# One order table for every engine's share of a piece, a PSUM bank table, and one copy for the gate transposes

## The chip, the cores and the metric

The kernel runs on one core of a Trainium2 chip. Its time is the device time of one execution in microseconds. Five engines work in parallel, each through its own queue in program order: TensorE (PE in the profile, its weight loads PEld), VectorE (DVE), ScalarE (ACT), GpSimd (POOL) and SyncE (SP), which here issues the DMAs.

## The reference

The first half is a recurrence over 768 time steps for 4 batches of 8 heads, with a state of 40 by 40 for each. The second half is a gated MLP with a spatial mixing matrix over the 768 positions.

```python
for t in range(S):
    y[:, :, t] = np.einsum('bhd,bhde->bhe', rt, state)
    Sa = np.einsum('bhde,bhe->bhd', state, at)
    state_decay = state * wt[:, :, None, :] - np.einsum('bhd,bhe->bhde', Sa, bt)
    state = state_decay + np.einsum('bhd,bhe->bhde', vt, kt)
...
h = x @ w_in
h = 0.5 * h * (1.0 + np.tanh(c * (h + 0.044715 * h ** 3)))
u, v = (h[..., :d_ff // 2], h[..., d_ff // 2:])
v_n = (v - mu) / np.sqrt(var + 1e-06) * g_ln
v_s = np.einsum('ts,bsd->btd', w_sg, v_n) + b_sg[None, :, None]
return (x + (u * v_s) @ w_out).astype(np.float32)
```

## The kernel before

**Attention.** The recurrence is cut into 12 chunks of 64 steps, and a chunk into 4 batches b. For each chunk and batch the gates are made by eight pieces (lines 252 to 309): `gate_1` a scan of the decays (ex), `gate_2` the product at, a copy of it on ScalarE and a copy of the last decays (`call`) on GpSimd, `gate_3` and `gate_b` the scaled keys kb, `gate_4` the 16 score products into two PSUM banks and the four transposes of kb into the free halves of the same banks, `gate_a` the masked scores, `gate_n` their negated part (nts), `gate_k` two ScalarE copies of the transposes into kbt.

A chunk then needs the inverse of a triangular matrix of 32 by 32 blocks. `inv_in` (line 311) transposes nts into n and copies the identity into x; `steps` (line 320) are 31 steps of a product (tg) and a sum (x), each needing the one before. All but the last few steps run on GpSimd; `LASTS` says for each chunk how many go to VectorE. `train` (line 567) lays them out: the first `HALF` instructions of a chunk's train follow each other, the remaining ones alternate with the start of the next chunk's train. `inv_back`, `inv_g` and `inv_x` make the inverse of the 64 by 64 matrix (tiles x1z, xt, gp, xp).

The chunk itself is `chain1` to `chain5` (lines 425 to 509): products with the state (ru), with the inverse (ru again, vu), the new state (`chain3`: sp, 16 products of 32 columns of weights; `chain3b`: sc, vs), the outputs (pq, pqs, yp, yt) and their stores to xd in DRAM.

**MLP.** The weights come as 64-bit numbers. Each of 12 blocks of w_in and 8 of w_out is decoded by `split64` (line 711): a DMA into one of three staging buffers (stg), Abs on ScalarE (sc), four VectorE operations, two ScalarE operations (lt and the high half), and three operations for the low half on GpSimd or VectorE (`DEC`). Then for each batch `in_v` and `in_u` make products (hv, hu) and gelu (tiles p and q, six buffers shared by all of them and by sc and lt), `sgu` the spatial mixing (sg, g, split into gy and gx), `outp` the output (op, y). `product` issues the matmuls of one product; the other engines' share follows at lags given to `later` and is run by `tick`.

**The order.** Every instruction stands in its engine's queue in the order in which the program issues it (line 126 is where all of them are recorded, so every row of the profile has that line). The pieces of the attention and the early pieces of the MLP are put into a list with positions from hand-written tables (`CH`, `GPOS`, `DEC`, `DECO`, `START`, `BACK`), the list is sorted, and each piece is then run whole, so that all engines get their share of it at that point:

```python
        def merge(*lists):
            for _, f in sorted((x for l in lists for x in l), key=lambda x: x[0]):
                f()
```

PSUM has eight banks of 512 numbers for each partition. Six are taken in rotation by `Banks`, and two hold scan operands until the gates are done, after which the rotation is over eight.

Of the kernel before, what the change touches and what calls it, by code (L numbers as in the profile page):

```python
# [9 lines left out]
F32 = mybir.dt.float32  # L10
# [8 lines left out]
C = 64  # L19
# [8 lines left out]
RING = 18  # L28
# [3 lines left out]
GROWTH = 34  # L32
# [9 lines left out]
CH = ((0.15, 1.92, 4, 5.28, 4.96, 7.81, 8.16, 8.46, 12.17, 12.47, 3.28, 10.6, 13.17, 14.9), (-0.13, 1.6, 7.06, 5.51,  # L42
    8.56, 6.96, 8.97, 9.27, 11.23, 11.29, 2.43, 6.58, 12.67, 13.85))
GPOS = (((5.05, 5.33, 6.03, 6.08, 8.35, 10.4, 10.41, 10.42), (8.01, 8.01, 8.01, 9.58, 11.74, 11.88, 11.88, 11.89),
# [7 lines left out]
BACK = (23.33, 25.65, 29.14, 26)  # L52
# [5 lines left out]
DSTEP = ((-9.0, -1.0, 0.0, 0.7, 1.35, 2.4), (-9.0, -1.0, 0.0, 2.16, 3.15, 3.15))  # L58
# [10 lines left out]
FIRSTS = ('v0', 'v1', 'v2', 'u1', 'u0', 'u3', 'u2', 'v3', 'v4', 'v5', 'u4', 'u5', 'u7', 'u6')  # L69
# [3 lines left out]
REST = 8  # L73
SGS = (5, 5, 6, 6, 7, 8, 8, 11, 10, 11, 12, 11)
PO = 313.2
DECO = (332.78, 334.78, 336.78, 339.28, 340.91, 351.01, 348.0, 347.78)
DSTEPO = (-4.0, -1.0, 0.0, 0.7, 1.4, 2.4)
SGE = 'GGGGGVGVVVVV'
# [5 lines left out]
LASTS = (9, 0, 0, 0, 2, 1, 2, 1, 1, 1, 2, 2)  # L84
BEGIN = (14.05, 14.1, 14.15, 14.2, 14.3, 14.4, 14.5, 14.6, 14.7)
# [8 lines left out]
EX = ((0, 0.3, 0.6, 0.61, 1.5, 2.45, 2.46, 2.89), (0, 0.3, 0.6, 0.61, 1.5, 2.6, 2.61, 2.62))  # L94
class Banks:


    def __init__(self, tc, ctx):
        self.tc, self.ctx, self.n = tc, ctx, 0
        self.rings = [ctx.enter_context(tc.tile_pool(name="ps", bufs=6, space=PSUM))] * 6  # L100
# [6 lines left out]
    def grow(self):  # L107
        if len(self.rings) == 6:
            self.rings += [self.ctx.enter_context(self.tc.tile_pool(name="ps_more", bufs=2, space=PSUM))] * 2
# [1033 lines left out]
```

## Time and profile before

| | us |
|---|---|
| median of 3 runs | 642.31 (641.55 to 644.67) |
| the execution with the profile | 644.61 |
| its span, first to last instruction | 642.9 |
| busy in the span: TensorE | 546.6 |
| VectorE | 503.5 |
| ScalarE | 375.7 |
| GpSimd | 385.1 |

A busy time is the time in which an engine has an instruction under way; a wait is idle time before an instruction, put down to what released it. A row of a timeline that ends in x2 merges two instructions that follow each other. The chain that ended last is followed back from the last instruction, at each step to what released it.

### The profile page before, as it was taken

To read this page: it belongs to the slowest core of one execution; us is meant where nothing else is said; L and a number is where in the kernel's file an instruction comes from. 1 tells how busy PE (TensorE), PEld (TensorE's weight loads), DVE (VectorE), ACT (ScalarE), POOL (GpSimd) and SP (SyncE) were. 2 spreads that over 40 slices of the span, in tenths; PEclk is the share of its full clock that TensorE was granted. 3 is DMA by queue.
4 is the path that set the end of the run, shared out by engine and by line. 5 is a ranking of instruction groups with operands and counts; after the bars stand their busy time and mean duration, and the time that the engine had idled before them with its cause. 6 is when DMAs were issued, how large, how long until landed. Compare 5 with 4: busy or idle time off the path is not lost.

```text
span 642.9 us, 26868 instructions
## 1 busy us (share of the span) xinstructions
PE 546.6 (85%) x11190; PEld 486.6 (76%) x11190; DVE 503.5 (78%) x1061; ACT 375.7 (58%) x1058; POOL 385.1 (60%) x917
## 2 busy tenths in 40 slices
PE   6526888889898898888897965879999999999995
PEld 6315667777777786777786755779999999999995
DVE  7858888889898897888788769785689878668633
ACT  4526787787977788777776734653344345334400
POOL 5588688888888888788884555634241423343220
PEclk8556799999999998999887986969999999999999
DMA  8822334444444443433344242230016213000001
GB/s 258 240 63 64 95 101 113 115 122 120 109 112 114 125 127 95 109 97 101 83 139 141 76 140 67 90 110 8 25 44 196 87 57 104 1 32 12 19 32 37
DMA packets 60515, 60.77 MB, mean 95 GB/s; under 512 B 36256, under 2 KB 50336, under 8 KB 60384
## 3 DMA queue, kind: packets, MB, share of 16 engines
q1 hardware_dynamic: 60384, 58.96, 32.5%
q8 instruction: 90, 1.47, 1.0%
q14 instruction: 41, 0.34, 0.2%
HBM read 51.07 MB, written 7.86 MB: 92 GB/s over the span
## 4 chain that ended last, share of the span: by engine, by line
PE 59%; DVE 20%; issue 7%; ACT 7%; POOL 4%; DMA 2%; DVEq 0%; SPq 0%; POOLq 0%; ACTq 0%
PE sg L126 16%; PE op L126 7%; PE ab L126 6%; PE pq L126 5%; PE hu L126 5%; PE hv L126 5%; PE yp L126 5%; PE ru L126 4%; DVE sc L126 3%; DVE at L126 2%; DVE fixed L126 2%; PE sp L126 2%; DVE stg L126 2%; POOL x L126 1%; PE ut L126 1%
## 5 line engine op out<-in xcount | busy, mean ns | idle before, releaser
L126 POOL TENSOR_TENSOR tg<-x,n 128x96 f32<-128x96 f32 (+15 forms) x351 | 130.5, 375 | 40.0 <-DVE fixed L126 7.3
L126 POOL TENSOR_TENSOR x<-x,tg 128x96 f32<-128x96 f32 (+15 forms) x351 | 133.5, 384 | 22.2
L126 POOL TENSOR_TENSOR gx<-g,gy 128x384 fp32r<-128x384 f32 x31 | 32.1, 1038 | 89.8 <-ACT gy L126 89.8
L126 PE MATMUL sg<-wsh,vh 128*128 128x384 f32 x192 | 66.3, 345 | 3.1 <-ACT vh L126 3.1
L126 PE MATMUL sg<-wsh,vl 128*128 128x384 f32 x192 | 66.6, 347 | 2.7 <-POOL vl L126 2.7
L126 ACT ACTIVATE nts<-ab 32x256 f32<-32x256 f32 x192 | 62.2, 324 | 9.9 <-DVE at L126 7.4
L126 PE MATMUL sg<-wsl,vh 128*128 128x384 f32 x192 | 65.9, 343 | 0.0
L126 PE MATMUL yp<-pqs,kbt 128*64 128x64 f32 x768 | 51.1, 235 | 14.6 <-DVE pqs L126 12.1
L126 PE MATMUL pq<-rt,vut 128*128 128x128 f32 x384 | 59.0, 299 | 1.5 <-issue 1.3
L126 PE MATMUL ab<-at,kb 64*64 64x64 f32 x1536 | 42.8, 244 | 20.1 <-DVE kb L126 9.9
L126 ACT CAST gy<-g 128x384 fp32r<-128x384 f32 x32 | 16.4, 514 | 74.2 <-DVE g L126 74.2
L126 PEld LDWEIGHTS ab<-at,kb 64*64 64x64 f32 x1536 | 34.2, 151 | 28.2 <-issue 8.5
L126 PEld LDWEIGHTS yp<-pqs,kbt 128*64 128x64 f32 x768 | 40.6, 145 | 17.8 <-DVE pqs L126 11.9
L126 PEld LDWEIGHTS pq<-rt,vut 128*128 128x128 f32 x384 | 49.9, 202 | 4.8 <-issue 1.8
L126 DVE TENSOR_TENSOR at<-ab,mask 64x256 f32<-64x256 f32 x96 | 36.0, 410 | 18.4 <-PE ab L126 18.0
L126 ACT CAST vh<-v 128x512 fp32r<-128x512 f32 x24 | 14.9, 620 | 57.2 <-DVE v L126 57.2
L126 PE MATMUL yp<-rt,s 80*40 80x64 f32 x704 | 47.0, 230 | 0.7 <-issue 0.7
L126 POOL TENSOR_TENSOR vl<-v,vh 128x512 fp32r<-128x512 f32 x24 | 31.3, 1306 | 22.6 <-ACT vh L126 22.6
L126 DVE SCALAR_TENSOR_TENSOR g<-sg,gl,bt 128x384 f32<-128x384 f32 x32 | 19.7, 615 | 28.1 <-PE sg L126 26.2
L126 ACT COPY vs<-sc 64x160 f32<-64x160 f32 x88 | 28.3, 321 | 21.1 <-DVE sc L126 20.2
L126 PEld LDWEIGHTS sg<-wsh,vh 128*128 128x128 f32 x192 | 37.0, 193 | 4.1 <-ACT vh L126 3.8
L126 PEld LDWEIGHTS sg<-wsh,vl 128*128 128x128 f32 x192 | 37.0, 192 | 3.9 <-POOL vl L126 3.9
(137 smaller groups left out, 1533.3 us busy)
## 6 DMA issues: line engine op xcount, KB each, us to landing
main<-main SPq DMA_DIRECT2D x88, 160.8 KB
vu<-vs SPq DMA_DIRECT2D x24, 160.0 KB
vs<-vb SPq DMA_DIRECT2D x24, 160.0 KB
rt<-rt SPq DMA_DIRECT2D x48, 80.0 KB
vut<-vt SPq DMA_DIRECT2D x24, 160.0 KB
xd<-yt SPq DMA_DIRECT2D x96, 40.0 KB
ws<-seq_w SPq DMA_DIRECT2D x20, 192.0 KB
xt<-xd SPq DMA_DIRECT2D x16, 192.0 KB
```

Source lines behind the costliest of these rows:

```text
L126: return self.tc.keep_in_program_order(f(*a, **k))
```

## The change

Each piece is cut into the shares of its engines, written as generators or lists of functions. `Plan.put` names each share, and `ORDER` gives every name a rank: 3862 entries from the first gate to the last output. `Plan.run` sorts by rank. So a share of VectorE can stand far from the TensorE share of the same piece, and instructions of two trains, the copies of decays, DMA issues and the four parts of `chain5` have places of their own. `BANKS` names the PSUM bank of each allocation in turn.

`gate_4` keeps the 16 score products; the four transposes become `gate_t` with a bank of their own, which `gate_k` reads with one copy. `chain3` makes 8 products of 64 columns of weights instead of 16 of 32. The tiles p and q of gelu get two buffers each (`PB`), sc and lt four of half the size (`CB`). Some of the lists change: `LASTS`, `HALF`, `AE` (one product at goes to GpSimd), `CLAMPO` (three clamps go to GpSimd), `GROWTH`, and positions.

In `ORDER`, the train instructions are the entries sp (products) and ss (sums); the decoding is wi and wo, whose low halves stand behind the last train instruction (rank 2516, from rank 2553 on); the shares of `chain4` and `chain5` are c4 and c5. The mask of the last chunk's last batches has ranks 2954 and 2988, the first step behind Square of the three filler products 2955, 2963 and 2995, their products 2892, 2896 and 2965 among the last chunk's outputs (2887 to 3008). The low halves of the two w_out blocks 5 and 6 end at 3280 and 3281, behind the first spatial products (3167 and 3168). The table and the functions that are only cut into shares are shortened here:

```diff
-GROWTH = 34
+GROWTH = 37
...
-DEC = ((270.96, 0), (275.26, 0), (280.96, 0), (285.42, 0), (296.05, 1), (295.96, 0), (300.96, 0), (305.96, 1),
+DEC = ((270.96, 0), (275.26, 0), (280.96, 0), (285.42, 0), (295.34, 1), (295.96, 0), (300.96, 0), (305.96, 1),
...
-CLAMPO = (0, 0, 0, 0, 0, 0, 0, 0)
+CLAMPO = (0, 1, 0, 0, 1, 1, 0, 0)
...
-DECO = (332.78, 334.78, 336.78, 339.28, 340.91, 351.01, 348.0, 347.78)
+DECO = (332.78, 334.78, 336.78, 339.28, 340.91, 348.2, 348.0, 347.78)
...
-LASTS = (9, 0, 0, 0, 2, 1, 2, 1, 1, 1, 2, 2)
+LASTS = (11, 0, 0, 0, 2, 0, 0, 1, 1, 1, 2, 2)
...
-AE = ('VVV', 'VVV', 'V', 'V')
-HALF = (40, 54, 54, 54, 54, 54, 53, 53, 52, 54, 54, 54)
-LEAD = (0, 0, 0, 0, 0, 0, 0, 0, 0, 0, 0, 0, 0)
+AE = ('VVG', 'VVV', 'V', 'V')
+HALF = (40, 54, 51, 51, 52, 54, 52, 53, 49, 54, 51, 54)
+LEAD = (0, 0, 0, 0, 0, 0, 0, 3, 0, 0, 0, 0, 0)
...
+PB, CB = 2, 4
+INTRO, LATE = -100, 500
+V_AT = ((0, 5), (0, 6), (1, 5.5), (1, 6.5), (1, 7), (1, 8), (1, 9), (1, 9), (2, 7.5), (2, 10), (2, 10))
+U_AT = ((0, 5), (0, 6), (1, 5.5), (1, 6.5))
+S_AT = ((0, 6),) * 4
+O_AT = ((0, 6),) * 2
+L_AT = ((-1, 0), (-1, 0), (-1, 0), (-1, 0), (-1, 0), (-1, 0), (-1, 0), (-1, 0), (-1, 0), (-1, 0), (-1, 0))
+ORDER = {
+    "g0": (0, 13, 37, 43, 82, 84, 139, 147, 266, 187, 279, 282, 320, 433, 461, 471, 512, 514, 696, 741, 716, 717,
...
+    "sp": (90, 92, 94, 96, 99, 101, 103, 105, 107, 109, 111, 113, 115, 117, 119, 121, 123, 125, 127, 129, 201,
...
+        1532, 1534, 1536, 1538, 1540, 1542, 1545, 1549, 1554, 1556, 1551, 1560, 1553, 1564, 1559, 1568, 1563,
...
+    "ss": (91, 93, 95, 98, 100, 102, 104, 106, 108, 110, 112, 114, 116, 118, 120, 122, 124, 126, 128, 202, 203,
...
+        1533, 1535, 1537, 1539, 1541, 1543, 1547, 1550, 1555, 1558, 1552, 1561, 1557, 1566, 1562, 1570, 1565,
...
+    "ni": (75, 89, 190, 200, 357, 364, 579, 587, 794, 795, 1063, 1070, 1287, 1302, 1492, 1493, 1724, 1734, 1951,
...
+    "vl": (3696,),
+    "rest": (3050, 3153),
...
+    "l1": (3850, 3851, 3852, 3853, 3854, 3855, 3856, 3857, 3858, 3859, 3860, 3861),
+}
...
+BANKS = ("0123450301253534125053210205435104132514513014253045213501420143015130124515240303251404325043125242"
...
+        k = int(self.order[self.n]) if self.n < len(self.order) else self.n % len(self.pools)
         self.n += 1
-        return self.rings[self.n % len(self.rings)].tile([128, 512], F32, tag="ps", name=nm)
+        return self.pools[k].tile([128, 512], F32, tag=f"bank{k}", name=nm)
...
+class Plan:
+
+
+    def __init__(self, order):
+        self.items, self.order = [], order
+
+    def put(self, pos, key, *fs):
+        self.items += [(pos, f"{key}.{k}", f) for k, f in enumerate(fs)]
+
+    def parts(self, pos, key, n, g, *a, **kw):
+
+        run = []
+
+        def part():
+            if not run:
+                run.append(g(*a, **kw))
+            next(run[0], None)
+
+        self.put(pos, key, *[part] * n)
+
+    def run(self):
+        ranks = {k: iter(v) for k, v in self.order.items()}
+        todo = [(next(ranks[key.split(".")[0]]) if ranks else pos, f) for pos, key, f in self.items]
+        for _, f in sorted(todo, key=lambda x: x[0]):
+            f()
...
-            ab = gate[c, b] = ps("ab0"), ps("ab1")
...
+    def banks(c, b):
+        if (c, b) not in scores:
+            scores[c, b] = ps("ab0"), ps("ab1")
+        return scores[c, b]
...
+    def gate_4(c, b):
+        kb, at, ab = gate[c, b], ats[ent(c, b)], banks(c, b)
+        for p in range(NP):
             for h in range(2):
-                V.tensor_tensor(out=at[0:64, :, h], in0=ab[h][0:64, 0:256].rearrange("p (q x) -> p q x", x=C),
-                                in1=mask[0:64].unsqueeze(1).broadcast_to([64, NP, C]), op=ALU.mult)
-
-        def gate_n(c, b):
-            nt, q0 = nts[c % 3], 4 * b
-            for h in range(2):
-                r, abv = 64 * h, gate[c, b][h][:, 0:256].rearrange("p (q x) -> p q x", q=NP)
+                r = slice(64 * h, 64 * h + 64)
+                for x in range(2):
+                    T.matmul(ab[h][64 * x:64 * x + 64, C * p:C * p + C], lhsT=kb[r, p, x], rhs=at[r, p, 1],
+                             start=True, stop=True, tile_position=(64 * h, 64 * x), skip_group_check=True)
+
+    def gate_t(c, b):
+        kb, kt = gate[c, b], ps("kt")
+        kts[c, b] = kt
+        for p in range(NP):
+            T.transpose(out=kt[:, 128 * p:128 * p + 128], in_=kb[:, p], identity=ident)
...
-        def gate_k(c, b):
-            for g in range(2):
-                A.copy(out=kbts[ent(c, b)][:, 160 * g:160 * g + 160].rearrange("p (q h x) -> p q h x", q=2, h=2),
-                       in_=gate[c, b][g][:, 256:512].rearrange("p (q h x) -> p q h x", q=2, h=2)[:, :, :, 0:D])
...
+    def gate_k(c, b):
+        A.copy(out=kbts[ent(c, b)][:, 0:DM].rearrange("p (q h x) -> p q h x", q=NP, h=2),
+               in_=kts.pop((c, b)).rearrange("p (q h x) -> p q h x", q=NP, h=2)[:, :, :, 0:D])
...
-        def chain3(c, b):
-            kbt, vu, sc = kbts[ent(c, b)], vus[b // 2][:, b % 2], scs[b]
-            if c < NCH - 1:
-                sp = ps("sp")
-                for p in range(NP):
-                    for x in range(4):
-                        h, r = x // 2, slice(32 * x, 32 * x + 32)
-                        l0 = 2 * D * p + D * h + 32 * (x % 2)
-                        T.matmul(sp[r, D * p:D * p + D], lhsT=kbt[:, l0:l0 + 32],
-                                 rhs=vu[:, p // 2, h, p % 2], start=True, stop=True, tile_position=(0, r.start))
-                ts = sums[b] = sp[0:e, 0:NP * D].rearrange("p (q x) -> p q x", x=D)
-                V.tensor_tensor(out=ts, in0=ts, in1=sc[0:e], op=ALU.add)
...
+    def chain3(c, b):
+        kbt, vu, sc = kbts[ent(c, b)], vus[b // 2][:, b % 2], scs[b]
+        sp = ps("sp")
+        for p in range(NP):
+            for h in range(2):
+                r, l0 = slice(64 * h, 64 * h + 64), 2 * D * p + D * h
+                T.matmul(sp[r, D * p:D * p + D], lhsT=kbt[:, l0:l0 + 64], rhs=vu[:, p // 2, h, p % 2],
+                         start=True, stop=True, tile_position=(0, r.start), skip_group_check=True)
+        ts = sums[c, b] = sp[0:e, 0:NP * D].rearrange("p (q x) -> p q x", x=D)
+        yield
+        V.tensor_tensor(out=ts, in0=ts, in1=sc[0:e], op=ALU.add)
...
+    PIECES = ((gate_1, 0), (gate_2, -1), (gate_3, 0), (gate_b, 2), (gate_4, 0), (gate_a, -1), (gate_n, -1), (gate_k, 0))
...
-        return self.sb.tile([128, HF], dt, name=nm, tag="pq", bufs=6)[:, 0:n]
+        if nm in ("p", "q"):
+            return self.pv.tile([128, HF], dt, name=nm, bufs=PB)[:, 0:n]
+        return self.sb.tile([128, HF // 2], dt, name=nm, tag="c", bufs=CB)[:, 0:n]
...
+    def work(self, plan, x, b, n, pos):
+
+        k = int(x[1])
+        g, a, steps = {"v": (self.in_v, (b, k), V_AT), "u": (self.in_u, (b, k % 4, k // 4), U_AT),
+                       "s": (self.sgu, (b, k % 4, k // 4), S_AT), "o": (self.outp, (b, k % 3, k // 3), O_AT),
+                       "l": (self.last_outs, (b, k), L_AT)}[x[0]]
+        run = []
+
+        def part():
+            if not run:
+                run.append(g(*a))
+            next(run[0], None)
+
+        plan.put(pos, f"{x}.{b}.m", part)
+        for i, (lag, rank) in enumerate(steps):
+            plan.put(self.late(n + lag) + 0.05 + 0.04 * rank if lag >= 0 else pos + 0.001 * i, f"{x}.{b}.{i}", part)
...
+        plan = Plan(ORDER)
+        verdict = attention(tc, a, xd, flag, keep, ps, plan)
+
+        def check(wm):
+            part.last = verdict(wm)
+
+        part.lay_out(plan, True, check)
+        plan.run()
+        part.ctx.close()
```

## Rows read from the trace of the kernel before

**Rows 1.** Busy time of each engine in four stages (window: length, then busy us of each).

```profile
21.35:62.00 40.65, 19.03 (x478) 15.27 (x478) 30.44 (x71) 18.81 (x58) 34.38 (x93) 0.52 0.38 99
62.00:345.60 283.60, 246.25 (x8548) 207.39 (x8548) 241.14 (x516) 222.29 (x691) 234.98 (x658) 0.97 0.42 110
345.60:423.50 77.90, 56.72 (x841) 48.91 (x841) 60.49 (x136) 45.02 (x121) 41.83 (x58) 0.82 0.37 106
423.50:635.80 212.30, 212.25 (x1153) 204.41 (x1153) 154.79 (x306) 78.84 (x159) 65.23 (x67) 0.99 0.17 52
```

**Rows 2.** Who GpSimd waited for, from 21 to 346 us (us, times, longest).

```profile
POOL tg L126 <- DVE n L126: 5.4, 5, 2.0
POOL tg L126 <- ACT rhsb L126: 4.5, 1, 4.5
```

**Rows 3.** Groups of GpSimd instructions, 21 to 346 us (busy, mean ns, idle before).

```profile
L126 POOL TENSOR_TENSOR x<-x,tg 128x96 f32<-128x96 f32 (+15 forms) x351 | 133.5, 384 | 22.2
L126 POOL TENSOR_TENSOR tg<-x,n 128x96 f32<-128x96 f32 (+15 forms) x351 | 130.5, 375 | 40.0 <-DVE fixed L126 7.3 <-DVE n L126 5.4 <-ACT rhsb L126 4.5
```

**Rows 4.** Timeline of GpSimd, one train alone (start, us).

```profile
22.08 0.24 POOL L126 TENSOR_TENSOR tg<-x,n 128x30 f32<-128x30 f32 x1
22.40 0.24 POOL L126 TENSOR_TENSOR x<-x,tg 128x30 f32<-128x30 f32 x1
```

**Rows 5.** Timeline of GpSimd, two trains in alternation.

```profile
73.63 0.48 POOL L126 TENSOR_TENSOR tg<-x,n 128x30 f32<-128x30 f32 x2
74.07 0.49 POOL L126 TENSOR_TENSOR x<-x,tg 128x30 f32<-128x30 f32 x2
```

**Rows 6.** Timeline of GpSimd, the end of chunk 0's train.

```profile
40.26 0.60 POOL L126 TENSOR_TENSOR tg<-x,n 128x121 f32<-128x121 f32 x2
...
42.62 0.29 POOL L126 TENSOR_TENSOR tg<-x,n 128x58 f32<-128x58 f32 x1
```

**Rows 7.** Timeline of GpSimd, the copies of decays.

```profile
152.34 0.56 POOL L126 COPY call<-ex 128x4 f32<-128x4 f32 x4
```

**Rows 8.** Timeline of GpSimd, decoding inside the last train.

```profile
341.56 0.88 POOL L126 TENSOR_TENSOR lt<-lt,sc 128x256 f32<-128x256 f32 x1
...
344.09 0.33 POOL L126 TENSOR_TENSOR tg<-x,n 128x56 f32<-128x56 f32 x1
```

**Rows 9.** Timeline of GpSimd, a product at made there.

```profile
8.23 0.68 POOL L126 TENSOR_TENSOR at<-main,ex 128x256 f32<-128x256 f32 x1
```

**Rows 10.** Who TensorE waited for, from 62 to 346 us.

```profile
PE ru L126 <- issue: 8.1, 11, 1.3
...
PE gp L126 <- DVE x1z L126: 3.7, 3, 2.8
...
PE sp L126 <- issue: 2.0, 2, 1.5
PE ab L126 <- ACT kbt L126: 1.8, 1, 1.8
```

**Rows 11.** The chain that ended last, in order of time (start, us, what).

```profile
227.83 1.07 PE yp L126 x32
...
236.10 0.42 PE sp L126 x32
```

**Rows 12.** Groups by shape: the copy of a gate's transposes (busy, mean ns, idle before).

```profile
L126 ACT COPY kbt<-ab 128x160 f32<-128x160 f32 x96 | 23.4, 295 | 0.7
```

**Rows 13.** Who VectorE waited for, from 346 to 424 us.

```profile
DVE sc L126 <- ACT sc L126: 6.2, 2, 4.4
DVE q L126 <- ACT p L126: 4.9, 6, 1.2
```

**Rows 14.** Timeline of TensorE, the last chunk's last output.

```profile
392.50 0.48 PE L126 MATMUL yp<-pqs,kbt 128*64 128x64 f32 x4 [7.40 <-DVE pqs L126]
```

**Rows 15.** Groups by shape: Square of a v and the step behind it.

```profile
L126 DVE SCALAR_TENSOR_TENSOR q<-p,hv 128x512 f32<-128x512 f32 x24 | 16.4, 682 | 10.4 <-ACT p L126 10.4
...
L126 ACT ACTIVATE p<-hv 128x512 f32<-128x512 f32 x24 | 14.3, 598 | 4.0 <-PE hv L126 2.8 <-POOL wol L126 1.0
```

More of the change, by code (lines that the diff above doesn't have):

```diff
@@ L51 @@
 E0K = 'GVVV'
[L52 removed]
+BACK = (23.33, 25.65, 29.2, 26)
 GX = (25.5, 4.6)
@@ L403, in inv_x, with inv_g @@
+    def inv_g(c):
+        nt, gs, x1z = nts[c % 3], gss[0], x1_of[c]
+        gp = ps("gp")
+        for q in range(8):
             for y in range(2):
@@ L565, in attention @@
-        rest = []
-        def train(c, n=0):
-            old, new = list(rest), steps(c, n, 31 - LASTS[c], G, (0, 16), f"tg{c % 2}") if c < NCH else []
-            k = HALF[c] if c < NCH else 0
-            rest[:], new = new[k:], new[:k]
-            order, old = old[:LEAD[c]], old[LEAD[c]:]
-            while old and new:
-                order += [old.pop(0), new.pop(0)]
-            return order + old + new
-        def first_loads():
-            return [(FL, lambda f=f, x=x: x(0, f)) for f in range(2) for x in (load_vb, load_rv)]
@@ new lines, in early, with both @@
+    def early(c, at, X, EA, EK, w):
+        for b in range(len(EA)):
+            gates(c, b, at + w * b, [w * x for x in X], EA[b], EK[b])
+    def both(c, n, at, w, nm="tv"):
+        first = steps(c, 0, n, V, (0, 16), nm)
+        lo, fs = at + w * (len(first) + 1), train(c, n)
+        plan.parts(at, f"ni.{c}", 2, inv_in, c)
+        for k, (key, f) in enumerate(first):
+            plan.put(at + w * (k + 1), key, f)
+        for k, (key, f) in enumerate(fs):
+            plan.put(lo + TW[c] * k, key, f)
@@ new lines, in attention, with train @@
+    rest = []
+    def train(c, n=0):
+        old, new = list(rest), steps(c, n, 31 - LASTS[c], G, (0, 16), f"tg{c % 2}") if c < NCH else []
+        k = HALF[c] if c < NCH else 0
+        rest[:], new = new[k:], new[:k]
+        order, old = old[:LEAD[c]], old[LEAD[c]:]
+        while old and new:
+            order += [old.pop(0), new.pop(0)]
+        return order + old + new
+    Q.dma_start(out=x0, in_=a["x0"])
+    for f in range(2):
+        load_vu(0, f)
+    bl = blanks()
+    early(0, INTRO, EX[0], E0A, E0K, 1.0)
@@ new lines, in attention @@
+    both(0, 0, INTRO + T0, 0.01)
+    early(1, INTRO + T2, EX[1], "VVVV", "VVVV", EW)
+    both(1, 0, INTRO + SECOND, 0.01)
+    early(2, INTRO + THIRD, EX[1], "VV", "VV", EW)
+    spread("zero", zeros(), INTRO + ZERO, INTRO + ZERO + 1)
+    spread("blank", bl, INTRO + TB0, INTRO + TB1)
+    for f in range(2):
+        plan.put(INTRO + FL, f"fl.{f}", lambda f=f: load_vb(0, f), lambda f=f: load_rv(0, f))
+    at = (INTRO + x for x in BEGIN)
+    z = next(at)
+    for key, f in steps(0, 31 - LASTS[0], 31, V, (0, 16), "tv"):
+        plan.put(z, key, f)
@@ L619, in verdict @@
+    plan.put(LATE - 0.95, "end.a", ctx.close)
     def verdict(wm):
@@ new lines, in store, with weights @@
+        def store():
+            Q.dma_start(out=self.out[b, mc, c], in_=y[0])
+        return ops, y, sums, store
+    def weights(self, plan, i, pos, steps, gens, flags):
+        for k, (p, g) in enumerate(zip(pos, gens)):
+            d = steps[flags[k]] if flags else steps
+            n = iter((1, 1, 2, 2, 2, 3))
+            fs = g()
+            j = 0
+            for x in d:
+                for _ in range(next(n)):
+                    plan.put(max(PIN + 0.1, p + x) if i == "i" and p > PIN else p + x, f"w{i}.{k}.{j}", fs[j])
+                    j += 1
```

1173 lines of the change are left out of this document (593 added, 580 removed), and 243 rows, old and new, of tables (GPOS, ORDER).

## The prediction

> **What bounds the kernel now.** The execution with the profile took 644.6 us, of which the span is 642.9; the median of the runs shown is 642.3, so what is summed against the profiled execution is put 2.3 us lower at the end. I read first the busy time by stage [rows 1]; the first gates are made ahead of these windows. From 21.4 to 345.6 us the twelve inverses run on GpSimd, one train of steps after another, while the other engines do gates and chunks; from 62 us on TensorE is busy 246.3, VectorE 241.1, ScalarE 222.3 and GpSimd 235.0 of 283.6 us, so shares alone name no bound. From 345.6 to 423.5 us the last chunk, the decoding of the weights and the first products of the MLP overlap; VectorE is busy 60.5 of 77.9. From 423.5 to 635.8 TensorE is busy 212.25 of 212.3: no order of the other engines can make that stage shorter. The last 7 us are the last sum and store.
>
> The second view settles the long stage: what GpSimd waited for. Between 21 and 346 us it waited 5.4 us for the transposed n of the next chunk and 4.5 us once behind a ScalarE copy [rows 2], and the rest of its unbusy time is small: the two groups of train instructions are 133.5 and 130.5 us busy with 22.2 and 40.0 us of idle before them [rows 3]. That is mostly the gap of some 0.06 us before each of 702 instructions, each of which needs the one before. GpSimd never pauses otherwise: the trains set the pace of the chunks, and the other engines follow. So I cost the change on GpSimd up to 345.6, on VectorE from there to 423.5, and on TensorE behind.
>
> **The trains of the inverse.** The table gives every product and every sum of a train its own place. Counting the full lists: before, 576 of 702 train instructions stand directly behind one of their own train; after, 552 of 704 when the copies of decays are left out. An instruction behind one of its own train starts 0.32 us after it at 30 columns [rows 4]; two trains in alternation start two such instructions every 0.44 us [rows 5]. A place in alternation thus saves 0.32 less 0.22, 0.10 us; 24 more save 2.4 us (0 if wide tiles hide their gap anyway, 5.3 if all of 0.22 went).
>
> The 48 copies of decays, now four in a row at 0.14 us each [rows 7], stand 43 times between two instructions of one train, where they lie in the gap that is there anyway. I take 0.05 us saved for each, near the gap of 0.06: 2.2 us; bounds 0 and 6.0 (43 times 0.14).
>
> Before, one block of the decoding (lt, stg, wil) stands on GpSimd ahead of the last four instructions of the last train: it holds the train from 341.56 to 344.09, 2.5 us [rows 8]. In the table all of these come behind the last train: 2.5 us saved for the last chunk.
>
> The list LASTS moves two steps (four instructions) of chunk 0 to VectorE and six instructions of chunks 5 and 6 back to GpSimd. The eight instructions from 40.26 to 42.62 [rows 6] are half chunk 0's: 1.2 us saved; the six added cost 0.22 each, 1.3 us; one product at of chunk 3 moves to GpSimd, 0.7 us [rows 9]. Net 0.8 us lost. VectorE gets its four in a stretch where it is busy 30.4 of 40.7 us [rows 1].
>
> The 9.9 us of waits at the joints of trains [rows 2]: HALF leaves more of the old train (11 instructions in chunks 2 and 3 where 8 were left) as filling while n is made, but a faster train also asks for n sooner. Unknown from both sides, 0 to 9.9 saved; I take half, 5.0, because the largest one lies where the table puts three more old instructions ahead of the new train.
>
> Sum on GpSimd: 2.4 + 2.2 + 2.5 - 0.8 + 5.0 = 11.3 us; with the lower bounds 1.7, with the upper ones 22.9.
>
> **How much of that arrives.** TensorE is the next engine in line. Beside its 246.3 busy us it stood in five groups of waits for nothing that the profile shows, from 8.1 down to 2.0 us, 21.3 us in all [rows 10]: 267.6 of 283.6 us. The change makes chain3's 16 narrow products into 8 of 64 columns: 32 records in 0.42 us become 16; the 128x64 products of yp, of 64 streamed columns, take 1.07/32 = 0.033 us a record [rows 11], 0.021 at 40 columns, so 0.33 us. That is 0.09 us for each of 44, 4 us in all (bounds 9 saved at today's rate a record, 5 lost at 0.033). TensorE then needs about 263.6 of some 272: 97%. Engines that run in order at that density lose some to each other, so I pass two thirds on: 7.5 us.
>
> On the waits without a visible releaser the Trainium skill says (Runtime: NRT & Kernel Launch, Instruction fetch mechanics) that the sequencer fetches its next block of instructions while it executes the present one and that crossing a block is mostly hidden. The trace has 21.3 us of such waits on TensorE and does not name their cause; if they were none of the engine's own need, all 11.3 us would arrive, and the time by it would be 642.3 - 11.3 - 8 (the next stage, below) = 623.0.
>
> **Gate transposes and banks.** The four transposes go to a bank of their own and one ScalarE copy of 320 columns reads them in place of two of 160. ScalarE saves a part of 48 copies; it is busy 222.3 of 283.6 us [rows 1] and stands on no path above, so I count nothing; were ScalarE the bound, it would be worth at most 48 times 0.295, 14 us [rows 12]. A gate now takes three banks instead of two of the six. TensorE waited 1.8 us, once, for a bank that the old copies read [rows 10]; the table picks banks so I take 0, with a loss of that size for each chunk (some 20 us) as the far end, which the slow half of the range holds in part.
>
> **The stage from 345.6 to 423.5.** VectorE idles 17.4 of 77.9 us there [rows 1], 6.2 of them for the size of weights that were still on their way and 4.9 for Square [rows 13], while TensorE waits 7.4 us for a mask of the last chunk that stands behind decoding and gelu on VectorE [rows 14]. The table puts that mask ahead of most of the first normalisation, lets the three filler products start among the last chunk's outputs, and moves two of the small w_out blocks behind the first spatial products. The work stays, so the gain is at most the idle time, 17.4; at least 0, if loads into the three staging buffers go on setting the times. I take nearly half, 8 us. The new loads and stores on SP's queue are hidden by DMA engines busy 0.37 of this stage; a late one shows as an idle VectorE again, which is the lower end.
>
> **The MLP stage.** TensorE has no idle time to give back: 0. Sum: 644.6 - 7.5 - 8 = 629.1, less 2.3: 626.8, say 627.
>
> **Rivals.** (a) All of the train's gain arrives and the transition gives 12: 642.3 - 11.3 - 12 = 619 or less. For it: the trains are the only bound the waits show. Against: TensorE at 97%. Chance 0.12. (b) TensorE becomes the bound of the chunks, more pieces and banks cost waits, the trains give 2 and the transition 4 to 5: 636. For it: the 21.3 us; against: its longest group of waits for another engine is 3.7 us today [rows 10]. Chance 0.14. (c) The joints of trains wait as long as before because n depends on gates, and the transition is set by its loads: 640 to 642, no change. Chance 0.09. (d) Slower: the MLP stage starves TensorE. The products p and q of gelu had six shared buffers and get two each; VectorE is busy 154.8 of that stage's 212.3 us [rows 1], and the way of a v through Square and the first VectorE step is 0.60 + 0.68 us [rows 15]. A third product cannot start its Square until the first's step is done; its PSUM bank then stays full and TensorE stops. There are 42 u and v products after batch 0. Against the 15.5 us saved this decides from 0.37 us a product; at 0.5 us it is 21 us lost, 648. For it: nothing idles before, so any wait counts in full; against: only 78.8 of 212 us of ScalarE are busy. Chance 0.10. That the table only repeats the old order is excluded by the counts above.
>
> **How the numbers follow.** The forecast (620 to 634) has 0.55, (a) 0.12, (b) 0.14, (c) 0.09, (d) 0.10. Within 0.5%, about what a measurement of this kernel tells from no change, is 639.1 to 645.5. Faster: 0.55 + 0.12 + 0.14 = 0.81; same 0.09; slower 0.10. A range from 612 to 641 leaves out (d), most of the upper half of (c) and the far end of (a).
>
> **What the profile would show.** Right: GpSimd still without pauses, its last train instruction at 334 to 339 us instead of 345.6; copies of decays singly between train steps; no decoding on GpSimd before that; the start of the gapless stage at 404 to 412 us; 212 us from there on. Wrong: TensorE waits for other engines between 62 and 340 us (b); waits for n at each joint (c); idle TensorE behind 430 us, with Square or PSUM as releaser (d).

## The result and the profile after

The changed kernel takes 623.36 us (median of 4 runs, 621.47 to 626.97) against 641.93 (4 runs, 639.05 to 644.67); the ratio is 0.9718, with a 95% interval of 0.9656 to 0.978. The profiled execution took 622.85 us, of which the span is 621.1, 21.8 less than before. Ratios and intervals, here and below, are of the fast executions alone, medians of all.

The busy time by stage, cut at the first and the last train instruction and at the start of the gapless stage (columns as in [rows 1]):

```profile
22.69:62.00 39.31, 16.25 (x508) 13.10 (x508) 35.90 (x85) 17.80 (x52) 33.23 (x90) 0.62 0.50 122
62.00:335.50 273.50, 242.90 (x7802) 206.45 (x7802) 229.72 (x505) 216.56 (x648) 235.88 (x666) 0.98 0.44 117
335.50:399.80 64.30, 52.94 (x842) 44.65 (x842) 56.13 (x121) 43.45 (x115) 41.18 (x56) 0.92 0.42 118
399.80:614.50 214.70, 213.89 (x1163) 205.27 (x1163) 160.49 (x318) 80.45 (x170) 70.90 (x76) 0.99 0.17 52
```

Against [rows 1] the trains begin 1.3 us later and are 11.5 shorter (312.8 where 324.3 were; 315.3 in a second execution, after_again), the stage behind them is 13.6 shorter (64.3, 77.9), and the MLP stage 2.4 longer. The store at the end is 0.5 shorter: 21.9 in all, the span's 21.8 but for rounding. Of the 2.4 us, 1.8 are only the cut: ten more products of 0.176 us lie behind it (x1163, x1153). The two stages together are 11.2 shorter.

What GpSimd waited for between the trains, from 24 to 345 us:

```profile
POOL tg L401 <- DVE n L401: 2.1, 3, 1.6
POOL tg L401 <- DVE ex L401: 1.1, 1, 1.1
POOL tg L401 <- ACT kbt L401: 0.8, 1, 0.8
```

4.0 us. [rows 2] have 9.9 before, but that view has a third row, a joint of trains too, which makes it 10.6:

```profile
POOL tg L126 <- ACT sc L126: 0.7, 1, 0.7
```

The timeline of GpSimd, a copy of decays between two steps and the end of the last train:

```profile
154.16 0.35 POOL L401 TENSOR_TENSOR tg<-x,n 128x96 f32<-128x96 f32 x1
154.46 0.19 POOL L401 COPY call<-ex 128x4 f32<-128x4 f32 x1
154.60 0.39 POOL L401 TENSOR_TENSOR x<-x,tg 128x96 f32<-128x96 f32 x1
...
335.23 0.27 POOL L401 TENSOR_TENSOR x<-x,tg 128x45 f32<-128x45 f32 x1
335.46 0.72 POOL L401 TENSOR_TENSOR lt<-lt,sc 128x256 f32<-128x256 f32 x1
```

Both are as the table has them: the copies of [rows 7] stand singly, with 0.09 us between the step before them and the sum behind it, and the decoding of [rows 8] follows the train's last sum instead of holding it.

The gapless stage begins here (timeline of TensorE):

```profile
399.76 0.45 PE L401 MATMUL sg<-wsl,vh 128*128 128x384 f32 x1 [4.18 <-DVE wsl L401]
```

### The profile page after: what moved, and what is told of

Same layout as the page of the kernel before. It is cut to its first block, busy times and chain, and to the rows that moved or that the text cites. A ratio compares the mean times of both kernels' runs of the same rounds, so it can differ in the third digit from the quotient of the medians.

```text
span 621.1 us, 25285 instructions
## 1 busy us (share of the span) xinstructions
PE 539.3 (87%) x10486; PEld 480.6 (77%) x10486; DVE 497.3 (80%) x1057; ACT 368.4 (59%) x1010; POOL 389.7 (63%) x923
## 4 chain that ended last, share of the span: by engine, by line
PE 47%; POOL 22%; DVE 16%; issue 8%; ACT 5%; DMA 1%; POOLq 0%; DVEq 0%; ACTq 0%
PE sg L401 13%; POOL x L401 10%; POOL tg L401 10%; PE op L401 6%; PE yp L401 5%; PE hv L401 4%; PE hu L401 4%; PE pq L401 4%; PE ru L401 3%; PE ab L401 2%; DVE v L401 2%; PE kt L401 2%; PE sp L401 2%; DVE n L401 1%; DVE q L401 1%
## 5 line engine op out<-in xcount | busy, mean ns | idle before, releaser
L401 POOL TENSOR_TENSOR tg<-x,n 128x56 f32<-128x56 f32 (+21 forms) x352 | 130.5, 375 | 30.2 <-DVE n L401 8.7
L401 POOL TENSOR_TENSOR x<-x,tg 128x100 f32<-128x100 f32 (+21 forms) x352 | 135.6, 389 | 20.1
L401 ACT ACTIVATE nts<-ab 32x256 f32<-32x256 f32 (+1 forms) x192 | 60.5, 322 | 16.4 <-PE ab L401 9.8
L401 ACT ACTIVATE q<-q 128x384 f32<-128x384 f32 (+1 forms) x56 | 31.4, 568 | 38.1 <-DVE q L401 36.2
L401 PE MATMUL ab<-at,kb 64*64 64x64 f32 x1536 | 38.1, 236 | 10.0 <-DVE kb L401 7.3
L401 PEld LDWEIGHTS ab<-at,kb 64*64 64x64 f32 x1536 | 31.0, 145 | 15.9 <-issue 4.4
L401 PEld LDWEIGHTS sg<-wsl,vh 128*128 128x128 f32 x192 | 36.5, 190 | 4.6 <-DVE wsl L401 4.4
L401 DVE TENSOR_TENSOR pqs<-pq,mask 128x512 f32<-128x512 f32 x48 | 32.5, 682 | 9.0 <-PE pq L401 8.8
L401 PE MATMUL kt<-ident,kb 128*128 128x128 f32 x192 | 33.4, 302 | 7.1 <-DVE kb L401 6.3
L401 PEld LDWEIGHTS yp<-rt,s 80*40 80x40 f32 x704 | 33.8, 121 | 5.9 <-ACT s L401 5.2
```

The source lines that it names most:

```text
L401: return self.tc.keep_in_program_order(f(*a, **k))
```

## The experiments

Each kernel's ratio is to the kernel before on the same chip (medians of before on the four chips used: 646.0, 643.6, 645.4 and 645.8 us). "Rest" is the time from the first train instruction to the end of the last, less the waits at joints, both from the profiled execution; of before it is 324.3 - 10.6. A joint is the place where one chunk's train gives way to the next one's.

| kernel | median us | ratio (95%) | last train end | waits at joints | rest |
|---|---|---|---|---|---|
| before | 641.9 | 1 | 345.6 | 10.6 | 313.7 |
| changed | 623.4 | 0.9718 (0.9656 to 0.978) | 335.5 | 4.0 | 308.8 |
| after_again | 625.3 | 0.9716 (0.9674 to 0.9757) | 337.6 | 7.6 | 307.7 |
| decode_in_train | 624.5 | 0.9682 (0.9642 to 0.9722) | 337.5 | 6.7 | 308.3 |
| one_after_other | 634.0 | 0.9816 (0.9779 to 0.9853) | 347.7 | 0 | 325.2 |
| copies_in_fours | 627.5 | 0.9731 (0.9688 to 0.9773) | 337.6 | 3.7 | 311.3 |
| two_copies | 627.1 | 0.9744 (0.9691 to 0.9797) | 341.5 | 11.0 | 308.2 |
| narrow_sums | 634.5 | 0.9844 (0.9813 to 0.9875) | 347.2 | 15.9 | 308.6 |
| before_wide_sums | 636.7 | 0.9896 (0.9866 to 0.9926) | 340.4 | 6.4 | 313.2 |
| mask_and_fillers_late | 630.5 | 0.9797 (0.9761 to 0.9834) | 337.5 | 7.7 | 307.3 |
| stores_in_piece | 668.1 | 1.0388 (1.0329 to 1.0446) | 363.7 | 24.8 | 316.4 |
| wide_chunks | 620.9 | 0.9656 (0.9616 to 0.9697) | 335.1 | 3.3 | 309.3 |
| wide_and_alternating | 632.2 | 0.9818 (0.9769 to 0.9867) | 344.0 | 22.2 | 299.2 |

In the diffs of the table an entry stands with its name in front of its rank.

**after_again.** No edit.

> The changed kernel itself, so that small differences are read against it on the same chip: 623 to 628 us, with the same stages as in its first profile within 1.5 us (train's last instruction at 335.5, gapless stage from 399.8). The waits at the joints of trains may differ by some us between executions.

The waits at joints differ by 3.6 us between two executions of one kernel, the rest by 1.1: so I read the rest to 1 us and the waits to 4.

**one_after_other.** Entries of the train's products and sums at the joints change places, 170 in all, as at the joint of chunks 1 and 2:

```diff
-    sp.2.0 398   sp.1.29 399   ss.2.0 400   sp.2.1 401   ss.2.1 402   sp.2.2 403   ss.1.29 404   sp.1.30 405
+    sp.1.29 398   ss.1.29 399   sp.1.30 400   ss.1.30 401   sp.2.0 402   ss.2.0 403   sp.2.1 404   ss.2.1 405
```

> The changed kernel, but each chunk's train on GpSimd ends before the next one begins; all other engines' orders are the same. 692 of 704 train instructions then stand behind one of their own train, instead of 552. Theory (the trains set the pace, and a dependent instruction costs 0.10 us more): the last train instruction ends 14 us later than in the changed kernel (335.5), at about 349, less what the joints give back, and the run takes 630 to 637. Rival 1 (wide tiles hide the gap): 335 to 338, the time stays at 623. Rival 2 (TensorE at 97% is the bound of the chunks): GpSimd gets slower, but the end moves by less than a third of what the steps lose.

The rest grows by 16.4 to 17.5 us, 0.12 for each of the 140 instructions. No wait at a joint is left to give something back, since n is there when it is asked for later. The train ends 10 to 12 us later, and in the profiled executions all of it arrives: the gapless stage begins at 412.87 instead of 399.76 and 400.74, 12 to 13 later. By the medians on one chip, 634.0 and the 624.5 of decode_in_train, whose order is the changed kernel's, 9.5 of 10.2 us arrive. Rivals 1 and 2 fall.

**copies_in_fours.** The 48 entries of the copies of decays:

```diff
-    "g1": (..., g1.1.0.3 390, ..., g1.1.1.3 369, ..., g1.0.0.3 382, ..., g1.1.2.3 416, ...
+    "g1": (..., g1.1.1.3 416, g1.0.0.3 416.1, g1.1.0.3 416.2, g1.1.2.3 416.4, ...
```

> The changed kernel, but the 48 copies of decays stand in twelve groups of four on GpSimd, as before the change. Theory (a copy between two steps lies mostly in their gap): 0.05 us for each of some 36 copies, 2 us, the train ends at about 337 and the run takes 625. Bounds: 0 (623) and 6 us (629).

The rest grows by 2.5 to 3.6 us, some 0.08 for each of 36. The ratios do not tell the two apart.

**decode_in_train.**

```diff
-    sp.11.27 2513   ss.11.27 2514   sp.11.28 2515   ss.11.28 2516
+    sp.11.27 2566.1   ss.11.27 2566.2   sp.11.28 2566.3   ss.11.28 2566.4
```

> The changed kernel, but one block of the decoding (three instructions on GpSimd) stands again ahead of the last four instructions of the last train. Theory: the train ends 2.3 to 2.5 us later (337.9) and the run takes as much longer, 625.5. Rival (the last chunk has slack behind the train): the train ends later, but the gapless stage of the MLP starts at 399.8 as in the changed kernel and the time stays at 623.

A miss of the edit: the block whose entries end at 2566 does its low half on VectorE, so no engine's order changed, and the three GpSimd instructions still came behind the train. It is a third execution of the changed kernel, and is used as that. The 2.5 us of [rows 8] were not tried alone.

**two_copies.**

```diff
-        A.copy(out=kbts[ent(c, b)][:, 0:DM].rearrange("p (q h x) -> p q h x", q=NP, h=2),
-               in_=kts.pop((c, b)).rearrange("p (q h x) -> p q h x", q=NP, h=2)[:, :, :, 0:D])
+        kt = kts.pop((c, b)).rearrange("p (q h x) -> p q h x", q=NP, h=2)
+        for g in range(2):
+            A.copy(out=kbts[ent(c, b)][:, 160 * g:160 * g + 160].rearrange("p (q h x) -> p q h x", q=2, h=2),
+                   in_=kt[:, 2 * g:2 * g + 2, :, 0:D])
```

> The changed kernel, but ScalarE reads a gate's transposes with two copies of 160 columns instead of one of 320. Theory (ScalarE stands on no path): the same time within 1 us, 622 to 624.5; ScalarE some 5 to 14 us busier. Rival (ScalarE bounds the chunks and the one copy brought part of the gain): up to 14 us longer.

Neither: the rest is the same, but the joints wait 11.0 us, 3 to 7 more than in three executions with one copy, and the train ends 4 to 6 later. The span, 623.9, is only 1.7 to 2.8 longer, the ratios overlap, and waits at joints are read to 4 us only. So the one copy may be worth some 2 us, but that is not shown. ScalarE's busy time rose by 2.6 to 3.6 us (372.0; 368.4, 368.7 and 369.4), less than the 5 to 14 expected.

**narrow_sums.**

```diff
-            for h in range(2):
-                r, l0 = slice(64 * h, 64 * h + 64), 2 * D * p + D * h
-                T.matmul(sp[r, D * p:D * p + D], lhsT=kbt[:, l0:l0 + 64], rhs=vu[:, p // 2, h, p % 2],
+            for x in range(4):
+                h, r = x // 2, slice(32 * x, 32 * x + 32)
+                l0 = 2 * D * p + D * h + 32 * (x % 2)
+                T.matmul(sp[r, D * p:D * p + D], lhsT=kbt[:, l0:l0 + 32], rhs=vu[:, p // 2, h, p % 2],
```

> The changed kernel, but chain3 makes its sums with sixteen products of 32 output partitions for each piece, as before, instead of eight of 64. Theory (TensorE is next in line, not the bound): TensorE's busy time from 62 us to the end of the train rises by 3 to 4 us, the train ends within 1.5 us of the changed kernel's, and the time within 2 us. Rival (TensorE bounds the chunks): 4 us longer or more.

The theory falls; the rival's 4 us or more came, though not through TensorE's busy time. The train ends 9.6 to 11.7 us later, the span is 11 to 12 longer, and the whole loss stands at the joints; by the ratios on one chip (0.9844, 0.9716) it is 8 us. What GpSimd waited for, 24 to 372 us:

```profile
POOL tg L401 <- ACT x L401: 11.7, 4, 3.9
POOL tg L401 <- ACT s L401: 2.2, 1, 2.2
POOL tg L401 <- DVE n L401: 1.3, 2, 0.8
POOL tg L401 <- ACT rhsb L401: 0.7, 1, 0.7
```

Most of it, 11.7 us, is put down to x, the copy of the identity on ScalarE, and not to n on VectorE. The largest but one of these waits, engine by engine (timelines of TensorE, VectorE, ScalarE and GpSimd):

```profile
147.64 0.31 PE L401 MATMUL yp<-rt,s 80*40 80x64 f32 x2 [1.28 <-issue]
...
145.65 2.12 DVE L401 STREAM_TRANSPOSE n<-nts 128x1024 f32<-128x1024 f32 x1
...
148.33 0.37 ACT L401 COPY vut<-ut 80x256 f32<-80x256 f32 x1 [2.83 <-PE ut L401]
148.60 0.62 ACT L401 COPY x<-x 128x512 f32<-128x512 f32 x1
...
149.30 0.24 POOL L401 TENSOR_TENSOR tg<-x,n 128x31 f32<-128x31 f32 x1 [3.57 <-ACT x L401]
```

TensorE comes to ut at 147.88, behind its wait of 1.28 us. ScalarE stands 2.83 us for ut, and the copy x, which takes no result of TensorE, stands behind that in ScalarE's queue: it ends at 149.22, n already at 147.77. In the changed kernel the same joint waits 1.13 us. So a late TensorE reaches the train through the queue of another engine, and x as well as n can come last.

What TensorE waited for from 62 to 335 us, here and in after_again:

```profile
PE ru L401 <- issue: 7.0, 11, 1.2
PE yp L401 <- issue: 4.1, 4, 1.6
PE ab L401 <- issue: 4.0, 5, 2.1
...
PE sp L401 <- issue: 2.7, 5, 0.7
PE xp L401 <- issue: 2.4, 5, 1.1
```

```profile
PE ru L401 <- issue: 8.0, 8, 2.4
...
PE xp L401 <- issue: 2.6, 3, 1.1
```

The waits for nothing that the profile shows are 20.2 us in these five groups and 10.6 in the two of after_again; with the small groups left out here, from 62 to 335 us each, 21.9 and 10.8, in the changed kernel 10.0, in the kernel before 24.6. The narrow products themselves were no dearer. Groups by shape, 62 to 335 us, narrow_sums and then after_again:

```profile
L401 PE MATMUL sp<-vu,kbt 128*32 128x40 f32 x1312 | 21.7, 205 | 3.1 <-issue 2.7 <-ACT kbt L401 0.4
```

```profile
L401 PE MATMUL sp<-vu,kbt 128*64 128x40 f32 x688 | 28.5, 230 | 0.7 <-ACT kbt L401 0.4
```

Sixteen narrow products are 16 x 21.7 / 1312 = 0.265 us of busy time, eight wide ones 8 x 28.5 / 688 = 0.331. The wide ones cost TensorE 0.07 us more a piece. What they gain goes with there being fewer products; that fewer weight loads or the width bring it is not told apart, as all three changed together.

**before_wide_sums.** The same edit the other way round, in the kernel before:

```diff
-                    for x in range(4):
-                        h, r = x // 2, slice(32 * x, 32 * x + 32)
-                        l0 = 2 * D * p + D * h + 32 * (x % 2)
-                        T.matmul(sp[r, D * p:D * p + D], lhsT=kbt[:, l0:l0 + 32],
+                    for h in range(2):
+                        r, l0 = slice(64 * h, 64 * h + 64), 2 * D * p + D * h
+                        T.matmul(sp[r, D * p:D * p + D], lhsT=kbt[:, l0:l0 + 64],
```

> The kernel before with one part of the change alone: chain3 makes its sums with eight products of 64 output partitions for each piece instead of sixteen of 32; 704 fewer products on TensorE. Theory 1 (fewer instructions on TensorE let the next chunk's n come in time at the joints): of GpSimd's 10.6 us of waits at joints 6 to 9 go, the train ends at 336 to 340 instead of 345.6, the run takes 633 to 637. Theory 2 (the prediction's: 4 us of TensorE, two thirds of what that frees): 639 to 641. Theory 3 (the new order alone needs them): no change.

Theory 1 in the time, and nearly at the train's end (340.4 where 336 to 340 were expected): the train ends 5.2 us sooner (and begins 0.6 sooner), the ratio is 0.9896, some 6.7 us. But the joints give only 4.2 of it, less than the 6 expected: one wait of 5.7 us for n is left. The rest is the old one, 313.2. TensorE's waits without a releaser fall from 24.6 to 10.6 us (62 to 335 us), and its busy time in the whole run rises from 546.6 to 552.5.

**wide_chunks.** Like this in `chain1` and, with `tile_position=(r.start, r.start)`, in `chain2`:

```diff
-            for x in range(4):
-                r = slice(32 * x, 32 * x + 32)
-                T.matmul(ru[r, D * p:D * p + D], lhsT=at[0:k, p, x // 2, 32 * (x % 2):32 * (x % 2) + 32],
-                         rhs=vs[0:k, p, x // 2], start=True, stop=True, tile_position=(0, 32 * x), skip_group_check=True)
+            for h in range(2):
+                r = slice(64 * h, 64 * h + 64)
+                T.matmul(ru[r, D * p:D * p + D], lhsT=at[0:k, p, h], rhs=vs[0:k, p, h],
+                         start=True, stop=True, tile_position=(0, r.start), skip_group_check=True)
```

> The changed kernel, and chain1 and chain2 make their products with 64 output partitions as well, in the way of chain3: 768 fewer products and weight loads, the same sums. Theory (each 700 fewer instructions free TensorE of some 10 us, in its busy time and in waits without a releaser, and the joints get n sooner): those waits fall from 11 to some 3 us, GpSimd's 4 to 8 us at the joints go to under 2, the train ends at 331 to 334, the run takes 617 to 622. Rival (the train's own 308 us of instructions are the bound by now): the train ends within 2 us of the changed kernel's.

What TensorE waited for without a releaser, 62 to 335 us:

```profile
PE yp L401 <- issue: 1.4, 1, 1.4
...
PE ru L401 <- issue: 1.0, 1, 1.0
...
PE xp L401 <- issue: 0.7, 1, 0.7
```

3.1 us, as the theory had it; yet the train ends where it did, as the rival said: 3.3 us of waits at joints are left to gain from and 309.3 are the train's own. So these waits are worth something only where they delay n or x. The ratio is 0.6% under that of after_again and 0.3% under that of decode_in_train, and the intervals overlap: it has the lowest median here, but is not told apart from the changed kernel.

**wide_and_alternating.** With `wide_chunks`, 162 train entries at nine joints, as at the joint of chunks 1 and 2:

```diff
-    ss.1.23 386   sp.1.24 387   ss.1.24 388   sp.1.25 389   ...   ss.1.28 397   sp.2.0 398   ...
+    sp.2.0 386   ss.1.23 387   ss.2.0 388   sp.1.24 389   ...   sp.2.1 391   ...   ss.1.28 408
```

> The wide chain1 and chain2, and on GpSimd nine of the eleven new trains start one to twelve pairs of steps sooner among the old train's last ones: 472 of 704 train instructions stand behind one of their own train, instead of 552; all other engines' orders are the same. Theory 1 (the train's own instructions, 308 us, are the bound): at 0.12 us for each of 80, which is what the 140 of the run with one train after the other cost, the train ends 9 to 10 us sooner, at 325 to 328, and the run takes 611 to 615. Theory 2 (trains and chunks run abreast: with wide products n was done 0.1 to 0.6 us before its first step at seven of the nine joints read): what the steps save is waited for n instead, the waits at joints rise from 3 to 10 us or more, the train ends at 334 to 337, 620 to 624 us.

The rest falls by 10.1 us, as 80 x 0.12 has it, and the waits eat it twice over. GpSimd's waits, and who waited for GpSimd (VectorE's waits, 62 to 340 us):

```profile
POOL tg L401 <- DVE n L401: 12.9, 3, 6.0
POOL tg L401 <- ACT rhsb L401: 9.3, 2, 6.1
```

```profile
DVE x1z L401 <- POOL x L401: 9.3, 3, 5.9
```

Theory 2, and worse: VectorE stands 9.3 us for the old train's x, where it stood 1.3 in wide_chunks. The likely reason is that the old train ends later for the new one's early steps, and that everything behind VectorE's wait, the next n too, is late for it.

**mask_and_fillers_late.**

```diff
-    c4.11.3.1 2988   c5.11.3.0 3005   c5.11.3.4 3023   u1.0.m 2980   u0.0.m 2992   u3.0.m 2993
+    c4.11.3.1 3028.5   c5.11.3.0 3028.52   c5.11.3.4 3028.6   u1.0.m 3028.58   u0.0.m 3028.585   u3.0.m 3028.59
```

> The changed kernel, but the mask of the last chunk's last output stands again behind two gelu steps and the first normalisation's statistics on VectorE, and the three first u products behind that output on TensorE, as before the change. Theory (the order at the last chunk's outputs brought most of the transition's 13.6 us): TensorE stands 6 to 8 us for that mask, its clock falls to 1.2 GHz there, the gapless stage starts 6 to 9 us later (406 to 409), 630 to 632 us. Rival (VectorE, busy 56 of 64 us there, sets the stage, and its own work is the same in any order): the wait appears, but the gapless stage starts at 399 to 402 and the time stays within 2 us.

Timeline of TensorE, and the busy time ahead of that product and behind it:

```profile
380.09 0.48 PE L401 MATMUL yp<-pqs,kbt 128*64 128x64 f32 x4 [6.44 <-DVE pqs L401]
```

```profile
372.00:380.00 8.00, 1.65 (x28) 1.37 (x23) 7.81 (x21) 4.95 (x13) 4.41 (x9) 0.83 0.45 118
378.00:384.00 6.00, 3.91 (x38) 3.75 (x39) 3.52 (x10) 0.88 (x3) 0.96 (x2) 0.50 0.25 65
385.00:390.00 5.00, 5.00 (x26) 4.52 (x26) 4.68 (x15) 3.40 (x10) 2.54 (x5) 1.00 0.82 259
```

TensorE stood for 6.44 us; its granted clock was 0.50, the lower level of 1.2 GHz, from 378 to 384 us and 1.00 from 385 on, where after_again has 1.00 in both stretches. The gapless stage begins at 404.38, 3.6 us later than in after_again with the train ending at the same time; by the ratios on one chip (0.9797, 0.9716) the run takes 5.2 us longer. So the theory had the wait and the clock right, but the stage's price is between the two; that VectorE, which goes on working in the wait, makes up for the rest is likely and was not tried. The three products moved here are the first u products. The three filler products of the prediction are v products: they stood among the last chunk's outputs already in the kernel before (371.07 to 378.1 us) and were not moved.

**stores_in_piece.** 96 entries; only SP's order differs:

```diff
-    "c5": (474, 475, 476, 477, 478, 533, 534, ...
+    "c5": (474, 475, 476, 477, 478, 478.01, 478.02, ...
```

> The changed kernel, but on SP's queue the two stores of each attention output stand right behind the VectorE step that makes it, as before, instead of at places of their own; only SP's order differs. Theory (SP stands for that step, and the loads behind it come late, most of all those of the weights in the last chunk): ScalarE and VectorE wait some us for a staged weight between the train's end and the gapless stage, which takes 67 to 72 us instead of 63.5 to 64.5; 627 to 633 us. Rival (the loads come early enough either way): the same time within 1.5 us.

The largest effect of all: 668.05 us, slower than before the change. What SP's queue, VectorE and TensorE waited for, 62 to 363 us, one fence each:

```profile
SPq L401 <- DVE yt L401: 83.4, 21, 8.7
```

```profile
DVE ex L401 <- DMA main<-main: 13.5, 6, 4.5
```

```profile
PE pq L401 <- DMA vut<-vt: 11.2, 4, 6.4
```

In the changed kernel, from 62 to 335 us, neither of the other two waits is there, and SP's for yt is:

```profile
SPq L401 <- DVE yt L401: 35.2, 11, 9.3
```

Of the 316.4 us of rest in the table, 6.7 are one wait of a copy of decays for ex. The trains end 28.2 us later than in the changed kernel, and the stage behind them takes 82.6 us (363.7 to 446.29) instead of 64.3. There ScalarE and VectorE wait for weights (363 to 440 us):

```profile
ACT sc L401 <- DMA stg<-w_out: 10.7, 3, 4.4
```

```profile
DVE sc L401 <- ACT sc L401: 15.2, 6, 4.7
```

In the kernel before, VectorE's wait of this kind was 6.2 us [rows 13]; in the changed one it is 1.4. The theory was right in kind and far too small in size. The kernel before has its stores in their pieces too, and SP stands only 22.3 us for yt there (62 to 346 us): the price is that of such stores in the new order, and not what the table saved against the old one.

**all_in_pieces.** 1110 entries of gates, chunk and inverse products move to their piece's earliest place (first piece of `c5`):

```diff
-    "c5": (474, 475, 476, 477, 478, 533, 534, ...
+    "c5": (474, 474.01, 474.02, 474.03, 474.04, 474.05, 474.06, ...
```

> The changed kernel, but in the attention every piece's shares (gates, chunk products, inverse products) stand together again at the place of the first share, on every engine; trains, decoding and MLP keep the table's places. Theory of the prediction (the trains set the pace; shares of other engines matter only where n comes late at a joint): the waits for n grow by the 5 to 6 us that the table saved there, the last train instruction ends at 341, and the run takes 630. Rival (a place of its own for each share is itself the gain of the chunks): TensorE, ScalarE and VectorE wait for each other in order, the train ends as late as before the change or later (346 and up), 635 to 645. Other rival: nothing depends on it, 335.5 and 623.

784.27 us, but it decides nothing. In eight gates the earliest place puts a reciprocal ahead of the scan that still needs the one before, so the sums of those gates change, and the order is not that of the kernel before either. What the shares' own places are worth on PE, ScalarE and VectorE stays open; on SP stores_in_piece shows it.

## Why the prediction was right, and where it was not

627.0 was forecast, 623.4 measured. The two parts were right in place and in sign, and both came out larger: 10.1 us at the train's end where 7.5 were passed on, 13.6 in the next stage where 8 were taken, less 2.4 in the last. Several steps in them were off, and two hits were luck.

**The train's own terms** nearly hold: pairs in alternation, copies, decoding and moved steps were summed to 6.3 us (2.4 + 2.2 + 2.5 - 0.8), and the rest fell by 4.9 to 6.0 (313.7 to 308.8, 307.7, 308.3). The price of a dependent instruction is 0.12 us by one_after_other and by wide_and_alternating, where 0.10 was read from [rows 4] and [rows 5]; that of a copy 0.08 instead of 0.05. At these prices the four terms would come to 8.0 (2.9 + 3.4 + 2.5 - 0.8), 2 to 3 more than the rest fell; where they went stays open (single slow steps, listed at the end, are of that size). Where the decoding now waits behind the train, the next is late as well: ScalarE stands 5.31 us for the low half that GpSimd has not yet read, and TensorE behind ScalarE (timeline):

```profile
337.20 0.44 PE L401 MATMUL yp<-rt,s 80*40 80x64 f32 x4 [5.08 <-ACT s L401]
```

Of these 5.08 us, 3.4 lie ahead of the train's end at 335.5.

**The joints**: 5.0 us were taken, 3.0 to 6.6 measured (10.6 to 7.6 and 4.0), but not for the reason given, more old steps as filling: that hit was luck. narrow_sums has the table, HALF and the filling, and its joints wait 15.9 us, more than before the change. The step that failed is the next one, where `chain3` was counted as 4 us less busy time of an engine that is not the bound. Its busy time rose, by 0.07 us a piece, 5.9 in the whole run of before_wide_sums, past the lower bound of 5 lost: a wide product was put at 0.021 us, scaled from yp's by its columns, and takes 0.041. What fell were TensorE's waits without a releaser, by more than half, and with them n and x came sooner. This one edit decides 9 to 12 us of the train in the new order, and 5.2 at its end in the old. On the train's length the two need each other: the order alone leaves it as it was (324.5 in narrow_sums, 324.3 before), the wide sums alone take 4.6, both together 9.0 to 11.5. In the whole time they nearly add up: 1.6% and 1.0% alone, 2.8% together, because the order alone already gives the stage behind the trains.

**How much arrives**: two thirds, for a TensorE at 97%. one_after_other and narrow_sums show all of it arriving in the profiled executions: 10 to 12 us at the train's end are 12 to 13 at the gapless stage. By ratios and medians on one chip it is 8 of 9.6 and 9.5 of 10.2, still more than two thirds. The sentence with the Trainium skill (Runtime: NRT & Kernel Launch, Instruction fetch mechanics) had all of it arrive, at 623.0, on the ground that TensorE has no need of its own for its waits without a releaser. The time agrees, but by luck: its 11.3 and 8 us were 10.1 and 13.6, less 2.4 in the last stage. And no run shows that ground: the waits went from 21.9 to 10.8 to 3.3 us as 704 and then 768 products, with as many weight loads, were dropped. That they fell each time is shown; that they are fetches is not, since the trace names no releaser.

**Gate transposes** were put at nothing; the one copy may bring some 2 us, which two_copies does not tell from noise, and no group of waits above 0.5 us that can be for a bank is to be seen in TensorE's list from 62 to 335 us.

**The stage behind the trains**: 8 us of VectorE's idle time were taken, and the stage is 13.6 shorter. VectorE's idle time fell by 9.2 (77.9 - 60.5 = 17.4 to 64.3 - 56.1 = 8.2), so the 8 were nearly right. The step that failed is "the work stays": VectorE's busy time in the stage fell by 4.4 us (60.5 to 56.1, x136 to x121), the other part of the 13.6. Seven steps of u products (13 with 7.2 us before, 6 with 3.2 now) and one small w_out block stand behind the start of the gapless stage now, where VectorE is busy 160.5 of 214.7 us, and three clamps are GpSimd's. What brought the idle time down is shown only in part: the mask and the first u products are 3.6 us of the stage. In the lists of VectorE's waits Square is gone (4.9) and the size of weights fell from 6.2 to 1.4, but one wait for the low half is new, 5.2 us, 1.2 of them behind the train's end:

```profile
DVE lt L401 <- ACT lt L401: 5.2, 1, 5.2
...
DVE sc L401 <- ACT sc L401: 1.4, 3, 0.7
```

TensorE's granted clock in this stage rose from 0.82 to 0.92, but that is not what made it shorter: narrow_sums has 0.83 there and takes 65.7 us. The sentence that SP's new loads and stores are hidden came true for the table's places, but the reason given, DMA engines busy 0.37, does not carry it: in stores_in_piece they are busy 0.38 of the stage and it takes 18.3 us more. What is scarce is SP's place in its queue, where a store that waits for VectorE holds every load behind it. How the idle time divides, the two w_out blocks among it, was not tried.

**The MLP stage** stayed as it was, 0 as forecast: 0.8 us of waits, beside the shifted cut.

**Rivals.** (a) is nearest to what happened: all or nearly all of the train's gain arrived, and the transition gave more than 12. Its 619 did not come because the trains begin 1.3 us later, which no step foresaw (the first n is transposed at 20.42 us instead of 19.10), and the last stage is 2.4 longer. (b) is wrong as a bound, yet right that TensorE's 21.3 us mattered; (c) fell, with 4.0 to 7.6 us at the joints; (d) fell, TensorE's waits behind 430 us are 0.8 us, for GpSimd.

## What to carry to other kernels

An engine that is "97% busy" beside a faster train may still be what makes the train wait: look at whose output ends the pace-setter's last waits, follow it back through the queues of the engines between, and count that engine's instructions, not only its busy time. On a queue that runs in order, DMA issues too, a store that waits for data is a wall for the loads behind it; give it a place after them. When two chains run abreast, a microsecond saved on one can be worth nothing until the other gives the same. And when a stage gets shorter, look whether its work got faster or only moved out of it.

## What the hardware showed unexpectedly

- TensorE's waits without a visible releaser fell with its number of products and weight loads, not with their busy time: 24.6 and 10.6 us in the old order, 21.9, 10.8 and 3.3 in the new one, in 273 us each.
- Products of 32 output partitions took 17 ns of busy time each where those of 64 took 41, with the same 40 streamed columns; twice as many of them still made the kernel 1.3% slower (0.9844 against 0.9716).
- 96 stores that stood some places earlier in SP's queue cost 43 us by the ratios (1.0388, 0.9718), with DMA engines busy some 0.4 of the time.
- Six single steps of a train took 0.83 to 1.50 us in the changed kernel, without a wait (1.11 at 328.51 us), where steps of their shapes take 0.39 to 0.47 on the mean in the kernel before, which has none above 0.8. VectorE was at work beside each of them; what made them slow no run shows.
